# The first loads on two queues and one epsilon on VectorE, in a fused layernorm, linear attention and gated layer

## Chip, cores and metric

The kernel runs on one core of a Trainium2 chip. The metric is the device time of one execution in microseconds (us). A core has five engines: TensorE (PE, matrix products), VectorE (DVE), ScalarE (ACT), GpSimd (POOL) and SyncE (SP, which here only issues transfers). They run their own instruction streams in order and wait for one another through semaphores. Transfers between HBM and the on-chip memory are done by 16 DMA engines; an engine that issues one puts it on its queue and goes on.

## What is computed

x is 2048 tokens by 512 channels in bf16. With xn = layernorm(x) the output is x + A(xn) + B(xn):

```python
xn = (x - mean(x)) / sqrt(var(x) + 1e-5)
# A: 32 heads of 16 channels, a learned feature map, linear attention
q, k, v = split(xn @ wqkv)
phi(t) = concat(softmax(t @ w_phi), softmax(-(t @ w_phi)))
o = phi(q) @ (phi(k)^T v) / (phi(q) @ sum(phi(k)) + 1e-6)
A = o @ wo
# B: bilinear gated layer, 512 -> 1792 -> 512
B = ((xn @ w_gate) * (xn @ w_up)) @ w_down
```

## The kernel before

The tokens are cut into 16 tiles of 128 (n = 0 to 15), four tiles to a group (GT = 4). Tile n lies in `xall[:, n, :]`, one token to a partition. Everything stays on chip: all weights are loaded once, and xn is kept transposed (channels on partitions) in `xnT`, which is what the projections and the gated layer read.

The order of the work on each engine is written out by hand (`manual_schedule`, L102): the instructions of an engine stand in the order in which the program emits them. All loads are issued by SyncE in one list ahead of that (L84 to L99): tile 0, tile 1, tiles 2 and 3, two halves of wv, the first two column blocks of w_gate and w_up (`dma_gu(0, 2)`), wphi, the next two blocks, the transposed k weights (wT2), and then the rest. Eight semaphores serve the loads in turn, so that the ninth load waits for the first, and so on.

While the first tile is on its way, TensorE runs ten matmuls on zeros (`warm_up`, L305 to L309), VectorE clears some buffers, GpSimd builds an identity matrix and a block mask, and ScalarE loads its activation table and runs one Exp on a constant (L106).

The layernorm of the first four tiles is done tile by tile:

- `ln_sums` (L153): bn_stats on VectorE (L155), tile `stats`.
- bn_aggr on VectorE (L347), tile `mv`: mean and variance.
- `ln_rstd` (L162): on GpSimd, variance plus epsilon (L164, tile `ve`), then the power of -0.5 (L166, tile `rstd`).
- `ln_apply` (L169): on VectorE, (x - mean) * rstd (L171, tile `xn`).

`first_stats` and `first_apply` (L340 to L355) set the order of these on VectorE: bn_stats and bn_aggr of tile 0, bn_stats and bn_aggr of tile 1, apply of tile 0, bn_stats of tile 2, apply of tile 1, bn_aggr of tile 2, and so on.

TensorE then transposes the tile (`lt`, L210 to L215): four transposes into PSUM (`tp`), which ScalarE copies into `xnT` (in two halves for tiles 0 and 1). Then come the v projection of tile 0 (`vproj`, L315; tile `pv`, L240), with the transposes of tile 1 put between its first two and its last two matmuls, that of tile 1, and the first units of the gated layer (`unit`, L268; tiles `g` and `u`, L275), which for the first two column blocks are done in two halves of tokens. After that the main loop mixes gated units, k, q and v projections, feature maps and the attention sums, so that TensorE always has matmuls at hand; tiles 4 to 15 are normalized in the background (`ln_block`) by VectorE, GpSimd and ScalarE and transposed by DMA. A last stage does the attention of each tile and the down projection (`fin`).

Of the kernel before, what the change touches and what calls it, by code (L numbers as in the profile page):

```python
# [11 lines left out]
ALU = mybir.AluOpType  # L12
# [9 lines left out]
def kernel(  # L22
# [12 lines left out]
    nc = tc.nc  # L35
    P = 128
# [7 lines left out]
    EPS = 1e-5  # L44
# [5 lines left out]
    def token_views(ap):  # L50
        rows = ap.flatten_outer_dims()
        first = rows[0:TT, :].rearrange("(n p) d -> p n d", p=P)
        rest = rows[TT:S, :].rearrange("(p n) d -> p n d", p=P)
        return lambda lo, hi: first[:, lo:hi, :] if hi <= GT else rest[:, lo - GT:hi - GT, :]

    x_view = token_views(A_x)
# [6 lines left out]
    xall = xpool.tile([P, NT, D], BF16)  # L63
# [10 lines left out]
    def dma_x(lo, hi):  # L74
        nc.sync.dma_start(out=xall[:, lo:hi, :], in_=x_view(lo, hi))
# [5 lines left out]
        dma_cols(nc.sync, wg, B_w_gate, lo * P, hi * P)  # L81
        dma_cols(nc.sync, wu, B_w_up, lo * P, hi * P)

    dma_x(0, 1)  # L84
    dma_x(1, 2)
    dma_x(2, 4)
    for lo in (0, 2):
        nc.sync.dma_start(out=wv[:, lo:lo + 2, :],
                          in_=A_wqkv[lo * P:(lo + 2) * P, 2 * D:3 * D].rearrange("(c p) f -> p c f", p=P))
# [58 lines left out]
    def bank(name, dt=F32, n=TT):  # L148
        return ps_s.tile([P, n], dt, name=name, tag="s")
# [3 lines left out]
    def ln_sums(n):  # L153
        stats = lnpool.tile([P, nc.vector.BN_STATS_DIM], F32, name="stats")
        nc.vector.bn_stats(out=stats[:], in_=xall[:, n, :])  # L155
        return stats
# [2 lines left out]
        stats = ln_sums(n)  # L159
        nc.vector.bn_aggr(out=mv, in_=stats[:])  # L160

    def ln_rstd(mv, k):  # L162
        ve = lnpool.tile([P, GT], F32, name="ve")
        nc.gpsimd.tensor_scalar(out=ve[:, 0:k], in0=mv[:, 0:k, 1], scalar1=EPS, scalar2=None, op0=ALU.add)  # L164
        rstd = lnpool.tile([P, GT], F32, name="rstd", bufs=GT)
        nc.gpsimd.tensor_tensor(out=rstd[:, 0:k], in0=ve[:, 0:k], in1=mhalf[:, 0:k], op=ALU.pow)  # L166
        return rstd

    def ln_apply(n, mean, rstd):  # L169
        xn = xnpool.tile([P, D], BF16, name="xn")  # L170
        nc.vector.tensor_scalar(out=xn[:], in0=xall[:, n, :], scalar1=mean, scalar2=rstd,  # L171
                                op0=ALU.subtract, op1=ALU.mult)
        xns[n] = xn

    def mv_tile():
        return lnpool.tile([P, GT, nc.vector.BN_AGGR_DIM], F32, name="mv", bufs=GT)
# [33 lines left out]
    def lt(n, parts=1):  # L210
        tp = bank("tp", BF16).rearrange("p (c t) -> p c t", c=DC)
        for c in range(DC):
            nc.tensor.transpose(out=tp[:, c, :], in_=xns[n][:, c * P:(c + 1) * P], identity=ident[:])  # L213
        for c in range(0, DC, DC // parts):
            nc.scalar.copy(out=xnT[:, c:c + DC // parts, n * P:(n + 1) * P], in_=tp[:, c:c + DC // parts, :])  # L215
# [3 lines left out]
    def make_bd():  # L219
        bo, wp = BO[:], wphi[:]  # L220
        nc.vector.tensor_tensor(out=bd[:], in0=_bcast_ap(bo, [bo.ap[0], [0, DC], [E1, 8], [1, DH]]),
                                in1=_bcast_ap(wp, [wp.ap[0], [DH, DC], [0, 8], [1, DH]]), op=ALU.mult)
# [15 lines left out]
    def proj(ps, n, w, js=range(DC)):  # L238
        for j in js:
            nc.tensor.matmul(ps, lhsT=xnT[:, j, n * P:(n + 1) * P], rhs=w[:, j, :],  # L240
                             start=(j == 0), stop=(j == DC - 1))

    def features(n, w, name):
        pf = bank(name)
        proj(pf, n, w)
        e = epool.tile([P, NG, 2, 4 * DH], F32, name="e")
        pfv = pf.rearrange("p (g c) -> p g c", g=NG)
        nc.scalar.activation(out=e[:, :, 0, :], in_=pfv, func=AF.Exp, scale=1.0)  # L248
        nc.scalar.activation(out=e[:, :, 1, :], in_=pfv, func=AF.Exp, scale=-1.0)  # L249
        ev = e[:].rearrange("p g s (h f) -> p (g s h) f", f=DH)  # L250
        sums = epool.tile([P, 2 * H], F32, name="sums")
        nc.vector.tensor_reduce(out=sums[:], in_=ev, axis=AX.X, op=ALU.add)  # L252
        rs = epool.tile([P, 2 * H, 1], F32, name="rs")
        nc.vector.reciprocal(out=rs[:].rearrange("p a b -> p (a b)"), in_=sums[:])  # L254
        phi = epool.tile([P, NG, P], BF16, name=f"phi{name}")
        nc.gpsimd.tensor_tensor(out=phi[:].rearrange("p g (x f) -> p (g x) f", f=DH), in0=ev,  # L256
                                in1=rs[:].to_broadcast((P, 2 * H, DH)), op=ALU.mult)
        return phi
# [52 lines left out]
    with tc.tile_pool(name="ps_k", bufs=1, space=PSUM) as ps_k:  # L311
        kvps = [ps_k.tile([P, 4, 4, E1], F32, name=f"kv{b}") for b in range(2)]
        phiks = {}

        def vproj(n, copy=nc.scalar.copy, amid=None, later=False):  # L315
            ps = bank("pv")
            proj(ps, n, wv, range(2))
            if amid is not None:
                amid()
            proj(ps, n, wv, range(2, DC))  # L320
            def evict():
                copy(out=vts[n % NV][:, :, :, 0:DH], in_=ps.rearrange("p (a b c) -> p a b c", a=8, b=4))  # L322
            if later:
                return evict
            evict()

        def kproj(n):
            phiks[n] = features(n, W1k, "k")

        def kv(n):  # L330
            vt, phik = vts[n % NV], phiks[n]
            for gr in range(NG):
                nc.tensor.matmul(kvps[gr // 4][:, gr % 4, :, :].rearrange("p a b -> p (a b)"),  # L333
                                 lhsT=phik[:, gr, :], rhs=vt[:, gr, :, :].rearrange("p a b -> p (a b)"),
                                 start=(n == 0 and gr % 4 == 0), stop=(n == NT - 1 and gr % 4 == 3))

        mvs = [mv_tile() for n in range(GT)]
        rstds = []

        def first_apply(n):  # L340
            ln_apply(n, mvs[n][:, 0, 0:1], rstds[n][:, 0:1])

        def first_stats(n, amid=None):
            stats = ln_sums(n)
            if amid is not None:
                first_apply(amid)
            nc.vector.bn_aggr(out=mvs[n][:, 0, :], in_=stats[:])  # L347
            rstds.append(ln_rstd(mvs[n], 1))

        first_stats(0)  # L350
        first_stats(1)
        first_apply(0)
        first_stats(2, amid=1)
        first_stats(3, amid=2)
        first_apply(3)  # L355
        make_bd()
        nc.gpsimd.tensor_tensor(out=M4[:], in0=BO[:, 0:4, :], in1=BO[:, 4:8, :], op=ALU.add)
        lt(0, parts=2)
        warm_up(1)
        vproj(0, amid=lambda: lt(1, parts=2))  # L360
        copy_v = vproj(1, later=True)
        lt(2)
        copy_v()
        unit(0, 0, 0, 2 * P)
        vproj(2, copy=nc.vector.tensor_copy, amid=lambda: lt(3))
        unit(0, 1, 0, 2 * P)
        vproj(3, copy=nc.vector.tensor_copy)
        for f in range(2):
            unit(0, f, 2 * P, TT)
        del units[0:2]  # L370
        ffn(1)
        for j0 in (0, 2):
            fold(1, W1k, j0, (nc.scalar.copy, nc.vector.tensor_copy))
        ffn(1)
        ln_block(4)
        ffn(1)
        chore(2)
        kproj(0)
        ffn(1)
        chore(2)  # L380
        ffn(1)
        chore()
        kproj(1)
        ffn(1)
        chore()
        ffn(1)
        kproj(2)
        chore()
        ffn(1)
        kv(0)  # L390
        chore()
        ffn(1)
        kproj(3)
        chore()
        ffn(1)
        kv(1)
        nc.sync.dma_start(out=wT2[:, 0, :, :], in_=A_wqkv[:, 0:D], transpose=True)
        for n in range(GT, NT):
            if n in (4, 8):
                ln_block(n + 4)  # L400
            vproj(n)
            kproj(n)
            chore(1 if n % GT < 2 else 0)
            ffn(1)
            kv(n - 2)
            chore((1, 2, 2, 2)[n % GT])
            if n >= 8 and n % 2 == 0:
                qproj((n - 8) // 2)
            if n == 6:
                fold(0, W1q, 0)  # L410
            ffn(1)
            if n == 6:
                fold(0, W1q, 2)
        ffn(1)
        kv(NT - 2)
        ffn(1)
        kv(NT - 1)
        for b in range(2):
            nc.vector.tensor_tensor(out=KV[:, 4 * b:4 * b + 4, :, :], in0=kvps[b][:],
                                    in1=_bcast_ap(M4[:], [M4[:].ap[0], [0, 4], [E1, 4], [1, E1]]), op=ALU.mult)  # L420
        qproj(4)
        ffn(1)
# [64 lines left out]
```

## Time and profile before

| | |
|---|---|
| median of 3 runs | 222.05 us (221.95 to 222.31) |
| the profiled execution | 221.94 us, of which the span of its instructions is 220.2 us |
| TensorE busy | 214.5 us (97% of the span) |
| VectorE busy | 138.4 us (63%) |
| ScalarE busy | 88.2 us (40%) |
| GpSimd busy | 72.1 us (33%) |
| DMA, mean over the span | 90 GB/s, 19.91 MB |

How to read the profile: one execution was recorded instruction by instruction. Times count from the first instruction of the span. PE stands for TensorE's matmuls, PEld for its weight loads, SPq for the instructions with which SyncE issues transfers. L155 is line 155 of the kernel before. The chain of work is followed back from the last instruction: at each step to whatever released it. "issue" in it is time in which the engine waited for nothing that the profile shows. A transfer is issued, moves its packets, and lands when its semaphore has its full count.

### The profile page before, as it was taken

Reading aid. Unit: us, or ns where it says so; the run is one execution under the profiler, and the core shown is the slowest. Engines: PE = TensorE matmul, PEld = TensorE weight load, DVE = VectorE, ACT = ScalarE, POOL = GpSimd, SP = SyncE. Lnnn points to the kernel's source line nnn. Section 1 sums busy time; section 2 is a strip of 40 time slices with the busy share of each in tenths; the row PEclk is TensorE's granted clock in tenths of the full one; section 3 lists DMA queues with packets and bytes.
Section 4 is the critical chain, followed back from the end, with each engine's and each line's share of the span. In section 5 each row is a group of like instructions: output and inputs, shape, how many; then the busy total and the mean of one; then the engine's idle time right before and its main releaser. Section 6 shows DMA issues by size and latency. Waiting matters only on the chain.

```text
span 220.2 us, 3489 instructions
## 1 busy us (share of the span) xinstructions
PE 214.5 (97%) x1285; PEld 104.4 (47%) x1309; DVE 138.4 (63%) x237; ACT 88.2 (40%) x162; POOL 72.1 (33%) x62
## 2 busy tenths in 40 slices
PE   7999999999999999999999999999999999999995
PEld 2564444445444444444544444444444444454443
DVE  5657985885579685756589964197655745445321
ACT  2635486559755876545354221231322323100000
POOL 5300555455336653536333633033033033000000
PEclk9999999999999999999999999999999999999999
DMA  5999994404201223010205945214431431522611
GB/s 171 261 306 383 368 225 59 95 1 49 49 0 33 42 54 65 18 34 0 48 1 100 119 95 113 58 24 95 98 72 24 95 71 27 91 53 71 69 30 48
DMA packets 47233, 19.91 MB, mean 90 GB/s; under 512 B 37488, under 2 KB 46960, under 8 KB 47088
## 3 DMA queue, kind: packets, MB, share of 16 engines
q1 hardware_dynamic: 47216, 19.69, 39.6%
q8 instruction: 10, 0.16, 0.3%
q14 instruction: 7, 0.06, 0.1%
HBM read 8.67 MB, written 2.10 MB: 49 GB/s over the span
## 4 chain that ended last, share of the span: by engine, by line
PE 94%; DVE 2%; DMA 1%; issue 1%; POOL 0%; ACT 0%; DVEq 0%
PE fin L293 22%; PE u L275 22%; PE g L275 21%; PE fin L296 6%; PE pv L240 6%; PE q L240 6%; PE k L240 6%; PE ab L430 2%; PE kv L333 2%; DMA xall<-in_A_x_dram 1%; DVE stats L155 1%; PE pq L231 1%; DVE sums L252 1%; PE tp L213 0%; DVE hT L280 0%
## 5 line engine op out<-in xcount | busy, mean ns | idle before, releaser
L275 PE MATMUL u<-xnT,wu 128*128 128x512 bf16 (+1 forms) x229 | 57.7, 372 | 0.4
L275 PE MATMUL g<-xnT,wg 128*128 128x512 bf16 (+1 forms) x222 | 56.7, 371 | 0.4
L280 DVE TENSOR_TENSOR hT<-u,g_sb 128x512 bf16<-128x512 f32 (+1 forms) x58 | 37.4, 649 | 27.3 <-PE u L275 18.0
L279 ACT CAST g_sb<-g 128x512 bf16<-128x512 f32 (+1 forms) x58 | 33.3, 573 | 48.2 <-PE g L275 48.1
L252 DVE TENSOR_REDUCE sums<-e 128x64 f32<-128x1024 f32 x32 | 38.9, 1215 | 20.7 <-ACT e L249 20.7
L293 PE MATMUL fin<-wd,hT 128*128 128x512 bf16 (+2 forms) x234 | 50.9, 366 | 0.3
L256 POOL TENSOR_TENSOR phiq<-e,rs 128x1024 bf16<-128x1024 f32 x16 | 31.0, 1935 | 61.4 <-DVE rs L254 53.1
L256 POOL TENSOR_TENSOR phik<-e,rs 128x1024 bf16<-128x1024 f32 x16 | 30.9, 1934 | 48.2 <-DVE rs L254 46.2
L275 PEld LDWEIGHTS <-wu 128*128 128x128 bf16 x232 | 22.6, 98 | 25.7
L293 PEld LDWEIGHTS <-hT 128*128 128x128 bf16 x238 | 22.4, 98 | 24.8
L275 PEld LDWEIGHTS <-wg 128*128 128x128 bf16 x232 | 21.9, 98 | 23.4
L240 PEld LDWEIGHTS <-xnT 128*128 128x128 bf16 x192 | 17.3, 97 | 18.2 <-ACT xnT L215 1.1
L299 DVE TENSOR_TENSOR o_sb<-fin,xall 128x512 bf16<-128x512 f32 (+2 forms) x17 | 11.2, 656 | 22.3 <-PE fin L296 22.2
L248 ACT ACTIVATE e<-q 128x512 f32<-128x512 f32 x16 | 9.5, 596 | 26.1 <-PE q L240 20.7
L254 DVE RECIPROCAL rs<-sums 128x64 f32<-128x64 f32 x32 | 17.7, 553 | 3.1
L240 PE MATMUL pv<-wv,xnT 128*128 128x512 bf16 x62 | 16.4, 379 | 0.4 <-ACT xnT L215 0.2
L296 PE MATMUL fin<-wo,oT 128*128 128x512 bf16 (+2 forms) x68 | 16.6, 366 | 0.0
L240 PE MATMUL k<-W1k,xnT 128*128 128x512 bf16 x63 | 16.2, 379 | 0.0
L240 PE MATMUL q<-W1q,xnT 128*128 128x512 bf16 x60 | 15.9, 378 | 0.1
L322 ACT CAST vt<-pv 128x512 bf16<-128x512 f32 x14 | 8.3, 591 | 10.9 <-PE pv L240 10.9
L248 ACT ACTIVATE e<-k 128x512 f32<-128x512 f32 x16 | 9.6, 597 | 7.0 <-PE k L240 6.6
L439 DVE TENSOR_TENSOR otok<-ab,rden 128x512 bf16<-128x512 f32 x16 | 11.1, 691 | 0.6
(46 smaller groups left out, 117.4 us busy)
## 6 DMA issues: line engine op xcount, KB each, us to landing
out_dram<-o_sb SPq DMA_DIRECT2D x15, 128.0 KB, 1.9
wd<-in_B_w_down_dram SPq DMA_DIRECT2D x1, 1792.0 KB, 15.4
wg<-in_B_w_gate_dram SPq DMA_DIRECT2D x2, 640.0 KB, 7.0
wu<-in_B_w_up_dram SPq DMA_DIRECT2D x2, 640.0 KB, 8.1
xall<-in_A_x_dram SPq DMA_DIRECT2D x1, 1024.0 KB, 12.0
wv<-in_A_wqkv_dram SPq DMA_DIRECT2D x2, 256.0 KB, 3.9
wg<-in_B_w_gate_dram SPq DMA_DIRECT2D x2, 256.0 KB, 4.9
wu<-in_B_w_up_dram SPq DMA_DIRECT2D x2, 256.0 KB, 5.3
```

Source lines behind the costliest of these rows:

```text
L240: nc.tensor.matmul(ps, lhsT=xnT[:, j, n * P:(n + 1) * P], rhs=w[:, j, :], start=(j == 0), stop=(j == DC - 1))
L248: nc.scalar.activation(out=e[:, :, 0, :], in_=pfv, func=AF.Exp, scale=1.0)
L252: nc.vector.tensor_reduce(out=sums[:], in_=ev, axis=AX.X, op=ALU.add)
L254: nc.vector.reciprocal(out=rs[:].rearrange("p a b -> p (a b)"), in_=sums[:])
L256: nc.gpsimd.tensor_tensor(out=phi[:].rearrange("p g (x f) -> p (g x) f", f=DH), in0=ev, in1=rs[:].to_broadcast((P, 2 * H, DH)), op=ALU.mult)
L275: nc.tensor.matmul(ps, lhsT=w[:, c, f * P:(f + 1) * P], rhs=xnT[:, c, T * TT + lo:T * TT + hi], start=(c == 0), stop=(c == DC - 1))
L279: nc.scalar.copy(out=g_sb[:, 0:hi - lo], in_=pss[0])
L280: nc.vector.tensor_tensor(out=hTs[T][:, f, lo:hi], in0=pss[1], in1=g_sb[:, 0:hi - lo], op=ALU.mult)
L293: nc.tensor.matmul(ps, lhsT=hTs[T][:, f, t4 * P:(t4 + 1) * P], rhs=wd[:, f, lo:lo + w], start=(f == 0), stop=False)
L296: nc.tensor.matmul(ps, lhsT=oTs[n][:, c, :], rhs=wo[:, c, lo:lo + w], start=False, stop=(c == DC - 1))
L299: nc.vector.tensor_tensor(out=o_sb[:], in0=ps, in1=xall[:, n, lo:lo + w], op=ALU.add)
L439: nc.vector.tensor_tensor(out=o_tok[:].rearrange("p (b h d) -> p b h d", b=2, d=DH), in0=abv[:, :, :, 0:DH], in1=rden[:].to_broadcast((P, ...
```

## The change

Tile 0 is loaded by two transfers of 64 partitions each, the first issued by SyncE and the second by ScalarE. Tile 1 is loaded by one transfer issued by ScalarE, behind that half. All other loads stay on SyncE in their order. For tile 0 alone the addition of epsilon is done by VectorE, directly behind its bn_aggr; the power stays on GpSimd. Both issues on ScalarE stand ahead of its table load. No arithmetic changes.

```diff
-    dma_x(0, 1)
-    dma_x(1, 2)
+    for eng, rows in ((nc.sync, slice(0, P // 2)), (nc.scalar, slice(P // 2, P))):
+        eng.dma_start(out=xall[rows, 0, :], in_=x_view(0, 1)[rows, 0, :])
+    nc.scalar.dma_start(out=xall[:, 1, :], in_=x_view(1, 2)[:, 0, :])
     dma_x(2, 4)
...
-    def ln_rstd(mv, k):
+    def ln_rstd(mv, k, eng=nc.gpsimd):
         ve = lnpool.tile([P, GT], F32, name="ve")
-        nc.gpsimd.tensor_scalar(out=ve[:, 0:k], in0=mv[:, 0:k, 1], scalar1=EPS, scalar2=None, op0=ALU.add)
+        eng.tensor_scalar(out=ve[:, 0:k], in0=mv[:, 0:k, 1], scalar1=EPS, scalar2=None, op0=ALU.add)
...
-        def first_stats(n, amid=None):
+        def first_stats(n, amid=None, eng=nc.gpsimd):
             stats = ln_sums(n)
             if amid is not None:
                 first_apply(amid)
             nc.vector.bn_aggr(out=mvs[n][:, 0, :], in_=stats[:])
-            rstds.append(ln_rstd(mvs[n], 1))
-
-        first_stats(0)
+            rstds.append(ln_rstd(mvs[n], 1, eng))
+
+        first_stats(0, eng=nc.vector)
         first_stats(1)
```

## The prediction

> **What bounds the kernel now.** I read the shares of the chain first, then the chain's first 7 us in order of time, then the same microseconds on each engine, then the landings of the loads. All times are from the profiled execution: span 220.2 us, device time 221.94 us, so 1.74 us lie around the span. The median of the runs is 222.05 us, 0.11 above it; I add that back at the end.
>
> The shares of the chain, by engine:
>
> ```profile
> PE 94%; DVE 2%; DMA 1%; issue 1%; POOL 0%; ACT 0%; DVEq 0%
> ```
>
> TensorE is the bound; some 6% of the chain is not TensorE. The chain in order of time (start, duration, what) shows where nearly half of that lies:
>
> ```profile
> 0.79 2.09 DMA xall<-in_A_x_dram
> 2.88 0.02 issue
> 2.90 0.71 DVE stats L155
> 3.61 0.02 issue
> 3.63 0.19 DVE mv L347
> 3.82 0.08 issue
> 3.90 0.25 POOL ve L164
> 4.15 0.07 issue
> 4.22 0.59 POOL rstd L166
> 4.81 0.03 issue
> 4.84 0.42 DVE xn L171
> 5.26 0.05 issue
> 5.31 0.41 PE tp L213 x4
> 5.72 0.02 issue
> 5.74 0.38 ACT xnT L215
> 6.12 0.05 issue
> 6.17 0.60 PE pv L240 x2
> ```
>
> Until 6.17 the end is set by tile 0 alone: its load, its statistics, the epsilon and the power on GpSimd, its normalization, its transposes and the first copy out of PSUM. From 6.17 on TensorE runs to 217.4 us almost without a hole, the larger apparent ones being matmuls whose records are missing. So a microsecond saved ahead of 6.17 is one saved at the end, if nothing else holds TensorE in the next 10 us.
>
> Two loads nearly do. The first half of pv for tile 0 needs the first piece of wv, the second half (6.99) the second, and u at 8.99 needs wu. Their issues (start, duration):
>
> ```profile
> 0.79 1.35 SPq L75 DMA_DIRECT2D xall<-in_A_x_dram  x3
> 2.18 0.98 SPq L88 DMA_DIRECT2D wv<-in_A_wqkv_dram  x2
> 3.20 0.47 SPq L78 DMA_DIRECT2D wg<-in_B_w_gate_dram  x1
> 3.72 0.51 SPq L78 DMA_DIRECT2D wu<-in_B_w_up_dram  x1
> ```
>
> The landing events of the trace put wv's pieces at 5.69 and 6.95, wg at 7.86, wu at 8.92. TensorE was free at 6.84 and took the second half of pv at 6.99, 0.04 after wv landed; but it then stood 0.04 for the copies of tile 1 (L215, 7.03 to 7.41) and began pv for tile 1 at 7.46. So the late wv cost nothing in the end: it could be later by only 0.02. u follows g without a hole at 8.995, and wu could have been 0.03 later. Any gain on tile 0's chain therefore counts only if wv and wu come earlier by nearly as much.
>
> **The change, part by part.**
>
> *Epsilon on VectorE.* It removes from GpSimd's path the 0.25 of L164 and a hop of 0.08. The power starts 0.09 after its input. VectorE has no 128x1 tensor_scalar in this trace; I bound it between the memset of 128x4 (62 ns) and the bn_aggr of 128x2 or the tensor_scalar of 128x32 (180 ns), and take 0.12, between two rows equally near. mv ends at 3.81; the epsilon starts 0.04 later (bn_aggr starts 0.03 after bn_stats), runs 3.85 to 3.97; the power runs 4.06 to 4.64 and would let xn go at 4.68, 0.16 before 4.84. But the epsilon stands on VectorE ahead of tile 1's bn_stats, and xn of tile 0 stands behind tile 1's bn_stats and bn_aggr:
>
> ```profile
> 3.63 0.18 DVE L347 BATCH_NORM_AGGREGATE mv<-stats 128x2 f32<-128x6 f32 x1
> 3.73 0.66 DVE L155 BATCH_NORM_STATS2 stats<-xall 128x6 f32<-128x512 bf16 x1
> 4.42 0.18 DVE L347 BATCH_NORM_AGGREGATE mv<-stats 128x2 f32<-128x6 f32 x1
> 4.84 0.41 DVE L171 TENSOR_SCALAR xn<-xall,mv,rstd 128x512 bf16<-128x512 bf16 x1 [0.23 <-POOL rstd L166]
> ```
>
> An instruction here can start 0.10 after bn_aggr started. Tile 1's bn_stats thus goes from 3.73 to 3.95, ends at 4.61, its bn_aggr starts at 4.65, and xn of tile 0 at 4.75. VectorE, not GpSimd, is late next: **0.09 us** gained of 0.33 taken out. Bounds: 0.16 if a dependent epsilon costs VectorE less, 0.00 if it takes 0.18 and nothing starts beneath it. Tile 1's own power moves from 5.09 to about 5.2 and its xn from 5.77 to 5.86, ended 6.25; TensorE wants it at about 6.4, so that is covered by 0.15.
>
> *Tile 0 in halves.* Each half is 64 KB. The issue takes 0.40 on SP, the first packets run at 1.82, each of the 16 engines needs 8 packets of 46 ns (0.37), the last engines finish near 2.5 and the last landing comes at 2.88. The halves use the same engines, so the 0.37 stays; what can shrink is the issue and the stagger of about 0.28 between the engines' first packets, each queue now preparing 64 rows and not 128. I take half of the stagger less something for the wait for the later of two: **0.10 us**. Bounds: the page's median of 1.9 us to landing for a 128 KB store against 1.4 for a 32 KB one allows 0.4 at most; a loss is priced under the rivals.
>
> The row above says that engine time is a small part of the 2.09. The Trainium skill, "DMA: Bandwidth & Descriptors", section "Rules for kernel authors", speaks against this part: two transfers to disjoint partition halves are not worth it, since both use the same 16 engines and serialize. By that rule this term is zero and the sum falls to the epsilon's 0.09; the 0.10 rests on latency outside the engines.
>
> *Tile 1 and x(2,4).* Tile 1's issue goes to ScalarE, second there, at about 1.24, as on SP now. bn_stats wants it at 3.95 less the 0.10; it now lands at 3.39. Beside x(2,4), which shares the engines from its first packet, it may lose the 0.35 that its own bytes take: 3.74. Just covered; if it came after 3.85 every 0.1 would delay xn of tile 0 by 0.1, since xn is behind that bn_stats.
>
> *The other loads.* All loads behind tile 1 on SP are issued one slot, 0.46, earlier. At present data waits for issues: by the trace's DMA packets the engines stand almost idle from 2.95 to 3.3 (10 KB in a quarter of a microsecond, against 96 at the busiest). The bytes ahead of wv and wu are the same, so closing that hole brings them 0.2 to 0.46 earlier, enough for a gain of 0.19 on the chain. wphi now waits for a half of tile 0 before its issue near 3.8; that landed a microsecond before.
>
> *ScalarE.* Two issues of 0.4 to 0.46 precede the table load (1.28 at 0.78 now), which then ends near 3.0, the first Exp at 3.2. The next work is L215 at 5.74: 2.5 us of cover, so nothing.
>
> **Sum.** 0.09 + 0.10 = 0.19 us off the profiled 221.94: 221.75; with the 0.11 of the median, **221.86 us**. TensorE's ten warm-up matmuls cap it: the last starts at 4.74 and takes 0.22, so tile 0's transposes, now at 5.31, cannot start before about 4.97, a cap of 0.34.
>
> About 0.2% (0.44 us) is what a measurement of this kernel can tell from no change. My forecast is within it.
>
> **Rivals.**
>
> *Halves bring nothing.* Both halves land at 2.88 as the one did. Only the epsilon counts: 222.05 - 0.09 = 221.96. For it: shared engines. Against: only 0.37 of 2.09 is engine time.
>
> *Chain gains up to the cap.* The halves land 0.25 or more sooner: 222.05 - 0.34 = 221.71.
>
> *The loads were the cost in the timed runs.* wv and wu stand 0.02 and 0.03 from holding TensorE in the execution profiled, and the runs reach 222.31, 0.37 over it. If ordinary runs lose 0.2 to 0.37 to a late wv or wu, the earlier issues remove it beside the chain's 0.19 to 0.34: 222.05 - 0.45 to 0.65, about 221.5. Against it: the median is only 0.11 above the profiled run.
>
> *ScalarE's queue is served late (the slower side).* First packets of the first three DMAs appear at 1.82, 2.59 and 3.3, 0.7 to 0.77 apart though issued 0.46 apart. If something common to both queues hands out DMAs at that pace, the second half of tile 0 starts near 2.59 and lands between 3.2 and 3.39, and tile 1, fourth in turn, at 4.2 to 4.5. xn of tile 0 then starts 0.25 to 0.65 later: 222.3 to 222.7, say 222.5. It decides from a landing of tile 0 past 2.97 or of tile 1 past 3.95. Against it: the engines take 96 KB in 0.25 us once fed, so no common pace of that size holds later.
>
> **Numbers.** Forecast 0.36, halves bring nothing 0.12, cap 0.08, loads 0.24, late queue 0.20, of which 0.04 stays within 0.2%. Faster is the loads' 0.24; slower 0.16; same 0.60. The range runs from 221.45, leaving out the best of the loads' case, to 222.50, leaving out the worse half of the late queue.
>
> **What would show it.** Right: tile 0's later half landing at 2.7 to 2.85; the power on GpSimd following VectorE by 0.09; xn of tile 0 near 4.65 directly behind tile 1's bn_aggr; first pv near 5.98 and TensorE full from there; wv and wu landing by 6.75 and 8.75. Wrong: VectorE waiting for tile 1's load; TensorE waiting at the second half of pv or at u; xn still waiting for the power; or the time around the span growing from 1.74 with a second queue in use.

## The result and the profile after

The changed kernel takes 222.55 us (median of 19 runs, 222.35 to 222.98) against 222.28 us before (19 runs, 221.95 to 222.64): a ratio of 1.0014, 95% interval [1.0008, 1.0021]. It is slower by about 0.3 us where 0.19 less was forecast, and lies 0.05 above the range. Part of the distance is the kernel before itself: over these 19 runs its median is 222.28, 0.23 above the 222.05 of three runs from which the forecast was reckoned. The sign is wrong by either count.

The profiled execution of the changed kernel took 222.98 us, the longest of its runs (span 221.2), while that of before was among the shortest of its own. The two traces differ by 1.04 us, the medians by 0.27, so the traces show where time goes, not how much of it. Each kernel was therefore profiled once more below (`before_again`, `after_again`).

The chain of waits of the changed kernel in its first profile (start, duration, what):

```profile
1.40 3.38 DMA xall<-in_A_x_dram
...
4.80 0.71 DVE stats L156
...
5.71 0.31 DVE xn L172
...
7.14 0.61 PE pv L241 x2
```

In this execution the chain runs through tile 1, not tile 0: a load of 3.38 us on ScalarE's queue, then bn_stats, bn_aggr and only then xn of tile 0. The first pv starts at 7.14 and not at 6.17. The same seen on VectorE, idle time ahead of an instruction in brackets:

```profile
3.22 0.69 DVE L156 BATCH_NORM_STATS2 stats<-xall 128x6 f32<-128x512 bf16 x1 [1.34 <-DMA xall<-in_A_x_dram]
...
4.80 0.69 DVE L156 BATCH_NORM_STATS2 stats<-xall 128x6 f32<-128x512 bf16 x1 [0.48 <-DMA xall<-in_A_x_dram]
...
5.62 0.38 DVE L172 TENSOR_SCALAR xn<-xall,mv,rstd 128x512 bf16<-128x512 bf16 x1
```

Tile 0's bn_stats starts at 3.22 against 2.90, and tile 1's waits 0.48 for its load. The issues, on SyncE and on ScalarE, in the same profile:

```profile
0.79 0.58 SPq L85 DMA_DIRECT2D xall<-in_A_x_dram  x1
1.42 0.57 SPq L75 DMA_DIRECT2D xall<-in_A_x_dram  x1
2.05 0.96 SPq L89 DMA_DIRECT2D wv<-in_A_wqkv_dram  x2
...
0.79 0.57 ACTq L85 DMA_DIRECT2D xall<-in_A_x_dram  x1
1.40 0.68 ACTq L86 DMA_DIRECT2D xall<-in_A_x_dram  x1
```

Half a tile is issued in 0.57 to 0.58 us where a whole one took 0.40, and the issues behind the halves are slow as well (0.68 on ScalarE, 0.57 on SyncE from 1.42). wv, which was to move from 2.18 to 1.72, moved to 2.05.

How the start carries to the end: the first pv of tile 1 starts at 7.46 in the first profile of before (221.94 us), 7.61 in its second (222.11), 8.26 and 8.43 in the two of the changed kernel (222.79 and 222.98), 8.73 in `e5_xn0_first` (223.29). The difference is 214.5 to 214.6 each time. In the other eleven profiles it is 214.4 to 214.9, most where wu came late and held u as well (`e7_halves_both_on_sp`, `e11_tiles23_halves`). Nearly all that follows is TensorE at work; the changed kernel's loss is made in the first 8 us.

### The profile page after: what moved, and what is told of

It reads as the page before. It is cut to its first block, busy times and chain, and to the rows that moved or that the text cites. A ratio compares the mean times of both kernels' runs of the same rounds, so it can differ in the third digit from the quotient of the medians.

```text
span 221.2 us, 3515 instructions
## 1 busy us (share of the span) xinstructions
PE 216.7 (98%) x1309; PEld 104.7 (47%) x1309; DVE 138.6 (63%) x238; ACT 88.1 (40%) x162; POOL 71.9 (32%) x61
## 4 chain that ended last, share of the span: by engine, by line
PE 96%; DMA 2%; DVE 1%; ACTq 0%; issue 0%
PE g L276 22%; PE fin L294 22%; PE u L276 22%; PE pv L241 6%; PE fin L297 6%; PE q L241 6%; PE k L241 6%; PE ab L431 2%; PE kv L334 2%; DMA xall<-in_A_x_dram 2%; PE tp L214 1%; PE pq L232 1%; DVE stats L156 0%; ACTq L85 0%; PE warm L308 0%; DVE xn L172 0%
## 5 line engine op out<-in xcount | busy, mean ns | idle before, releaser
L276 PE MATMUL g<-xnT,wg 128*128 128x512 bf16 (+1 forms) x232 | 57.9, 372 | 0.0
L156 DVE BATCH_NORM_STATS2 stats<-xall 128x6 f32<-128x512 bf16 x16 | 10.7, 669 | 1.8 <-DMA xall<-in_A_x_dram 1.8
```

What stands on the lines that cost most here:

```text
L276: nc.tensor.matmul(ps, lhsT=w[:, c, f * P:(f + 1) * P], rhs=xnT[:, c, T * TT + lo:T * TT + hi], start=(c == 0), stop=(c == DC - 1))
```

## The experiments

The first theory, drawn from the two traces, was Q: two queues that issue at once slow each other, and tile 1 comes late behind that. Two rivals stood against it: V, the epsilon itself delays VectorE, and C, the moment at which TensorE's clock rises makes the whole difference. "The clock rises" is short here for what the traces show of matmuls of 512 columns: up to some moment they start 0.43 us apart, and 0.22 apart after it. Every ratio is to the kernel before, run on the same chip. Code is cut to the lines that differ from the changed kernel, unless the text names the kernel before.

**The epsilon alone** (`e1_eps_only`): loads as before.

```diff
-    for eng, rows in ((nc.sync, slice(0, P // 2)), (nc.scalar, slice(P // 2, P))):
-        eng.dma_start(out=xall[rows, 0, :], in_=x_view(0, 1)[rows, 0, :])
-    nc.scalar.dma_start(out=xall[:, 1, :], in_=x_view(1, 2)[:, 0, :])
+    dma_x(0, 1)
+    dma_x(1, 2)
```

> All loads as before, only tile 0's epsilon on VectorE. Theory Q (the queues: two queues issuing at once take longer for each issue, and tile 1, second on ScalarE's queue, lands so late that VectorE waits for it ahead of xn of tile 0): this part is harmless, xn of tile 0 some 0.03 to 0.1 us earlier than before's 4.84, time 0.0 to 0.15 below before. Rival V (the epsilon ahead of tile 1's bn_stats delays VectorE by more than it saves): time 0.1 to 0.3 above before, VectorE the last to arrive at xn. Rival C (the profiled difference is TensorE's clock turning at another moment): no difference.

Measured: 222.29 against 222.30, ratio 1.0003 [0.9993, 1.0012]. This part loses nothing that can be told. The interval alone would leave room for V's 0.1 to 0.27 us, but on the chain the epsilon did what was forecast: xn of tile 0 starts 1.86 after tile 0's landing, against 1.96 in both profiles of before, so 0.10 is gained and V falls; the epsilon takes 154 ns on VectorE. But TensorE in this profile:

```profile
1.24 4.45 PE L307 MATMUL warm<-zeros 128*128 128x512 bf16 x10 [1.24 <-DVE zeros L104]
5.48 0.63 PE L213 MATMUL tp<-ident,xn 128*128 128x128 bf16 x4
```

The ten warm-ups end only here, at 5.48, with starts 0.43 apart to the last; xn was ready at 5.23 and waited. In the first profile of before they ended at 4.96: the ninth starts at 4.52, the tenth 0.22 behind it.

**The loads alone** (`e2_loads_only`): `first_stats(0)` without `eng=nc.vector`.

> The loads of the changed kernel, epsilon of all tiles on GpSimd. Theory Q: the whole loss is here, time 0.25 to 0.45 above before, tile 1 landing past 4.3 and bn_stats of tile 1 waiting for it. Rival V: time at or below before, since the loads would be the gain. Rival C: no difference.

Measured: 222.63, ratio 1.0017 [1.0008, 1.0027]. The loss is in the loads. But tile 1 landed at 3.84 and held nobody; tile 0 was complete only at 3.66, 0.78 later than in the first profile of before. So tile 1's 4.77 of the first profile after did not recur here, and tile 0 itself is late. Of Q's two signs the time came and the late tile 1 did not.

**Tile 1 back on SyncE** (`e3_tile1_on_sp`): halves as changed.

```diff
-    nc.scalar.dma_start(out=xall[:, 1, :], in_=x_view(1, 2)[:, 0, :])
+    dma_x(1, 2)
```

> Tile 0 in halves on the two queues, tile 1 back on SyncE behind its half; epsilon on VectorE. Theory Q: tile 0 still lands near 3.2 (its issues still meet), but tile 1, now ahead of tiles 2 and 3, lands by 3.6 to 3.8 and VectorE no longer waits for it; xn of tile 0 near 5.0; time 0.0 to 0.2 above before. If the late half of tile 0 is what costs and not tile 1: as the changed kernel, 0.25 to 0.4 above before. Rival V: 0.1 to 0.3 above before.

Measured: 223.03, ratio 1.0037 [1.0025, 1.005], worse than both, and more than any theory had asked. Tile 0 was complete at 3.20; VectorE no longer waited for tile 1, and the loss stayed. SyncE's second issue took 0.83 though ScalarE issued nothing beside it any more, wv went out at 2.81 and its second piece landed at 7.71. The chain has the first half of pv and its second half, which starts 0.04 after that landing and 1.25 behind the first half's start, where in before it was 0.82. The chain names ScalarE's copy of tile 1, which ended at the same moment, but this half reads tile 0 and wv:

```profile
6.50 0.60 PE pv L241 x2
...
7.75 1.46 PE pv L241 x6
```

**xn of tile 0 ahead of tile 1's statistics** (`e5_xn0_first`).

```diff
-        first_stats(1)
         first_apply(0)
+        first_stats(1)
```

> The changed kernel with xn of tile 0 placed on VectorE ahead of tile 1's bn_stats, so that nothing of tile 0 stands behind tile 1's load. Theory Q: tile 0's chain is then load, bn_stats, bn_aggr, epsilon, power, xn without a wait for tile 1: xn at about 5.0 against 5.62, and the time 0.1 to 0.35 below the changed kernel, unless tile 1's transposes then hold TensorE. Rival V: the same gain, for another reason, but e1 then is slower than before. Rival C: no difference to the changed kernel.

Measured: 223.29, ratio 1.0049 [1.0036, 1.0062], the slowest of all: a miss. xn of tile 0 came at 5.14 as expected, but tile 1's bn_stats stood behind it, its xn started at 7.40, and tile 1's transposes, between the two halves of pv, at 7.87. Tile 1 had landed at 3.93, so here there was no wait for its load to remove; the order costs more than it saves.

**Tile 0 whole on SyncE, tile 1 on ScalarE** (`e4_tile1_alone_on_act`).

```diff
-    for eng, rows in ((nc.sync, slice(0, P // 2)), (nc.scalar, slice(P // 2, P))):
-        eng.dma_start(out=xall[rows, 0, :], in_=x_view(0, 1)[rows, 0, :])
+    dma_x(0, 1)
     nc.scalar.dma_start(out=xall[:, 1, :], in_=x_view(1, 2)[:, 0, :])
```

> Tile 0 whole on SyncE, only tile 1 on ScalarE's queue, where it is first; epsilon on VectorE. Theory Q as it now stands (two issues made at once take 0.55 to 0.58 us and not 0.40, a next one on SyncE up to 0.83, so the slot that SyncE was to save is lost): SyncE's first two issues take 1.1 to 1.4 together, wv is issued at 2.05 to 2.3 and not 1.71; tile 1 lands by 3.4 together with tile 0, so VectorE doesn't wait for it; time between before and the changed kernel, 222.2 to 222.5. If a second queue in itself, not the meeting of issues, is the loss: as the changed kernel, 222.5 or more.

Measured: 222.76, ratio 1.002 [1.0011, 1.0029], as the expectation had it if a second queue in itself is the loss. Q's mechanism falls. The issues on both queues meet, and none is slow:

```profile
0.79 0.88 SPq L75 DMA_DIRECT2D xall<-in_A_x_dram  x2
1.72 0.97 SPq L88 DMA_DIRECT2D wv<-in_A_wqkv_dram  x2
...
0.79 0.39 ACTq L85 DMA_DIRECT2D xall<-in_A_x_dram  x1
```

First packets appear at 1.83 and 1.92 on the two queues. Still tile 0 lands late:

```profile
0.79 2.62 DMA xall<-in_A_x_dram
```

In before that line read 2.09. The packets of the two tiles run over the same stretch, from 1.83 to 3.05, and tile 0's last one comes at 3.00 against 2.53 in the first profile of before; both tiles finish late (3.41 and 3.60). The trace doesn't say which engine moved a packet, so that the two wait for each other on the engines is argued from these times, in one profile. wv left at 1.72, yet its second piece landed at 7.17: the earlier issue bought nothing.

**Both halves on SyncE** (`e7_halves_both_on_sp`): one queue only.

```diff
-    for eng, rows in ((nc.sync, slice(0, P // 2)), (nc.scalar, slice(P // 2, P))):
-        eng.dma_start(out=xall[rows, 0, :], in_=x_view(0, 1)[rows, 0, :])
-    nc.scalar.dma_start(out=xall[:, 1, :], in_=x_view(1, 2)[:, 0, :])
+    for rows in (slice(0, P // 2), slice(P // 2, P)):
+        nc.sync.dma_start(out=xall[rows, 0, :], in_=x_view(0, 1)[rows, 0, :])
+    dma_x(1, 2)
```

> Tile 0 in halves, both on SyncE, all other loads behind them there; epsilon on VectorE. Theory Q: with one queue each issue takes 0.40 again, also for half a tile; tile 0's second half is issued at 1.25 and lands near 3.2 to 3.4; all later loads one slot (0.46) later, so that wv's second piece lands near 7.3 and holds TensorE; time 0.2 to 0.5 above before. If a half issues and lands in clearly less than a whole (1.5 to 1.8 us after its issue): tile 0 complete by 2.9, time within 0.2 of before.

Measured: 223.20, ratio 1.0034 [1.0022, 1.0046]. The chain shows each issue:

```profile
0.79 0.58 SPq L85
...
1.42 0.57 SPq L85
...
2.04 0.59 SPq L75
...
2.68 0.42 SPq L75
```

With no second queue in use a half takes 0.58, and the issue right behind the halves, a whole tile, 0.59. The first half's first packet runs at 2.14 against 1.82, and it lands at 2.96: 64 KB alone arrive no earlier than 128 KB did. Part of the time lost here is the extra slot: wu landed at 10.12 and held u until 10.17, 0.3 after TensorE had come free. This gave theory H: a transfer of 64 partitions is slow in itself.

**Tile 0 cut by columns** (`e9_column_halves`), all else as changed.

```diff
-    for eng, rows in ((nc.sync, slice(0, P // 2)), (nc.scalar, slice(P // 2, P))):
-        eng.dma_start(out=xall[rows, 0, :], in_=x_view(0, 1)[rows, 0, :])
+    for eng, cols in ((nc.sync, slice(0, D // 2)), (nc.scalar, slice(D // 2, D))):
+        eng.dma_start(out=xall[:, 0, cols], in_=x_view(0, 1)[:, 0, cols])
```

> The changed kernel with tile 0 cut by columns (128 partitions x 256) and not by partitions. Theory H (a transfer of 64 partitions is itself slow to issue, 0.57 against 0.40 us, and brings its first packet 0.3 later, whatever the other queue does): each issue takes 0.40 or less, first packets near 1.85, tile 0 complete by 2.75 to 3.0, wv issued at 1.7; tile 1 lands between 3.4 and 3.9; time 222.1 to 222.45, at least 0.1 under the changed kernel. Rival S (two queues slow each other on the engines, however the tile is cut): tile 0 complete at 3.2 or later, time as the changed kernel's.

Measured: 222.44, ratio 1.0010 [1.0001, 1.0019]. Issues and first packets are as H says:

```profile
0.79 0.40 SPq L85 DMA_DIRECT2D xall<-in_A_x_dram  x1
1.24 0.44 SPq L75 DMA_DIRECT2D xall<-in_A_x_dram  x1
```

First packets run at 1.83 and 1.89. Tile 0 was complete at 3.15, later than H expected, perhaps since tile 1 and tiles 2 and 3 follow on two queues; tile 1 landed at 3.85. The time is below the changed kernel's as H asks, but the two intervals overlap, so the gain of 0.1 is not shown by the times alone.

**Column halves, tile 1 on SyncE, xn of tile 0 amid tile 1's statistics** (`e10_column_halves_amid`).

```diff
-    for eng, rows in ((nc.sync, slice(0, P // 2)), (nc.scalar, slice(P // 2, P))):
-        eng.dma_start(out=xall[rows, 0, :], in_=x_view(0, 1)[rows, 0, :])
-    nc.scalar.dma_start(out=xall[:, 1, :], in_=x_view(1, 2)[:, 0, :])
+    for eng, cols in ((nc.sync, slice(0, D // 2)), (nc.scalar, slice(D // 2, D))):
+        eng.dma_start(out=xall[:, 0, cols], in_=x_view(0, 1)[:, 0, cols])
+    dma_x(1, 2)
...
-        first_stats(1)
-        first_apply(0)
+        first_stats(1, amid=0)
```

> Tile 0 in column halves on the two queues, tile 1 back on SyncE behind its half, epsilon on VectorE, xn of tile 0 between tile 1's bn_stats and bn_aggr. Theory H: all loads but the second column half run as before, tile 0 complete by 2.75 to 2.9, tile 1 at about 3.4; time 221.9 to 222.2, the lowest so far, if halving can bring anything; 222.15, as with whole tiles in this order, if it can't. Rival S: tile 0 past 3.1, time above 222.3.

Measured: 222.66, ratio 1.0012 [1.0003, 1.0021]: a miss for H's hopeful side. Tile 0 was complete at 3.08, the half on SyncE last (its first packet at 2.11 against 1.81 on ScalarE). That is nearer to S (past 3.1, above 222.3) than to H. It also shows a first packet 0.3 late with all 128 partitions, so the late packet is not the partitions' alone when two queues are in use. Halving brings nothing even in the cheap form; in this profile wv's second piece landed at 7.53 and held pv besides.

**Tiles 2 and 3 in partition halves** (`e11_tiles23_halves`): the kernel before with only its third load cut.

```diff
-    dma_x(2, 4)
+    for rows in (slice(0, P // 2), slice(P // 2, P)):
+        nc.sync.dma_start(out=xall[rows, 2:4, :], in_=x_view(2, 4)[rows, :, :])
```

> The kernel before, tiles 0 and 1 whole on SyncE as ever, and only the third load (tiles 2 and 3) cut into two transfers of 64 partitions, both on SyncE: 128 KB each, as much as tile 0 whole. Theory H (the number of partitions makes an issue slow): both issues take 0.55 to 0.6 us, the issues behind them 0.75 later than before, wv's second piece past 7.5, time 0.3 to 0.8 above before. Rival B (what was slow was a small transfer, or the first one on an idle queue): 0.40 to 0.43 each, time 0.1 to 0.4 above before from one more slot.

Measured: 222.80, ratio 1.0025 [1.0012, 1.0038]. The chain, from the second issue on:

```profile
1.23 0.42 SPq L75
...
1.70 0.73 SPq L87
...
2.47 0.60 SPq L87
...
3.11 0.60 SPq L89
...
3.75 0.47 SPq L89
```

The halves carry 128 KB each and stand behind two whole tiles, and take 0.73 and 0.60; one more whole issue behind them is slow (0.60), then it is 0.47 again. The 0.73 is more than H's 0.55 to 0.6. Neither a small size nor first use makes an issue slow: with tiles 2 and 3 whole (128 partitions, 256 KB) it took 0.43, so the cut to 64 partitions does. wu landed 0.44 later than in the first profile of before, at 9.36, and held u until 9.41. That wv's second piece would come past 7.5 was a miss: 6.99.

**Both kernels once more** (`before_again`, `after_again`).

> The kernel before once more, one look. Theory W (the moment at which TensorE's clock rises differs between executions and makes most of before's spread): the ten warm-ups run at 0.43 us until a rise at some other moment than 4.4; if the rise comes after 5.5, tile 0's transposes start at 5.48 and not when xn is ready, and the time is 222.2 to 222.6; tile 0 lands again between 2.85 and 3.0.

> The changed kernel once more, one look. Theory H: halves issued in 0.57, tile 0 complete at 3.0 to 3.7, wv issued past 2.0. If the clock rises earlier than in the first profile (7.0), the time is 222.35 to 222.6, with xn of tile 0 still 0.4 or more behind before's. Rival C (the whole difference between the first two profiles is the clock): xn of tile 0 near 4.9.

Measured: 222.11 and 222.79. Before again, tile 0's transposes on TensorE:

```profile
5.46 0.39 PE L213 MATMUL tp<-ident,xn 128*128 128x128 bf16 x4
```

Tile 0's bn_stats and xn, before and after:

```profile
2.94 0.69 DVE L155 BATCH_NORM_STATS2 stats<-xall 128x6 f32<-128x512 bf16 x1 [1.05 <-DMA xall<-in_A_x_dram]
...
4.87 0.41 DVE L171 TENSOR_SCALAR xn<-xall,mv,rstd 128x512 bf16<-128x512 bf16 x1 [0.23 <-POOL rstd L166]
```

```profile
3.50 0.69 DVE L156 BATCH_NORM_STATS2 stats<-xall 128x6 f32<-128x512 bf16 x1 [1.62 <-DMA xall<-in_A_x_dram]
...
5.34 0.38 DVE L172 TENSOR_SCALAR xn<-xall,mv,rstd 128x512 bf16<-128x512 bf16 x1
```

Before, the transposes start at 5.46 though xn was ready at 5.28: the tenth warm-up, begun at the low rate at 5.05, came first, and the clock rose while it ran. After again, the first matmuls of pv:

```profile
6.98 0.59 PE L241 MATMUL pv<-wv,xnT 128*128 128x512 bf16 x2 [0.17 <-DMA wv<-in_A_wqkv_dram]
```

The clock thus rose at another moment than 4.4, as W has it, though not late enough for the 222.2 named. In after again the halves took 0.58 and 0.55 to issue, wv went out at 2.30, and the clock rose between 6.2 and 7.0. Tile 0 was complete at 2.91 before and 3.40 after; xn of tile 0 started at 4.87 and 5.34, 0.47 apart; rival C, which wanted 4.9, falls as the whole cause. pv then waited 0.17 for wv's first piece, which landed at 6.94 (5.80 before), so that in this execution the loads behind tile 0 cost too. Tile 1 landed at 3.72 and held nobody.

**What the clock hides** (`e8_before_8_warmups`, `e6_xn0_amid`, `e12_amid_9_warmups`). The first is the kernel before with `warm_up(8)`; the other two have before's loads, the epsilon on VectorE, and

```diff
-        first_stats(1)
-        first_apply(0)
+        first_stats(1, amid=0)
```

the last of them with `warm_up(9)`.

> The kernel before with 8 in place of 10 warm-up matmuls. Theory W (in ordinary executions TensorE's clock rises late, the warm-ups run at 0.43 us each until 5.5 and cover tile 0's chain up to there; the profiled execution of before was one with an early rise): the end of the warm-ups moves to 4.65, the median falls by 0.05 to 0.3, the fastest stay. Rival: the warm-ups never bind, and two fewer either change nothing or let the clock rise later: median equal or above.

> Loads as before, epsilon on VectorE, and xn of tile 0 placed between tile 1's bn_stats and bn_aggr. xn of tile 0 then waits for the power and comes 0.16 us before where it stood against tile 0's landing. If the ten warm-up matmuls at the low clock, which end at 5.48 in some executions, hide such gains: median 0.0 to 0.1 below before, the fastest runs 0.1 or more below before's fastest. If VectorE's chain is the bound in ordinary runs: 0.15 below before throughout.

> Loads as before, epsilon on VectorE, xn of tile 0 amid tile 1's statistics, and 9 in place of 10 warm-ups. Theory W (the end of the warm-ups covers what tile 0's chain gains): the warm-ups end by 5.05 at the latest, tile 0's transposes start 0.05 behind xn in every execution, median 0.1 to 0.3 below before. Rival: the clock rises later for the missing one and takes it back, or some executions near 224 as with 8 warm-ups: median 0.1 below before or less.

Measured: 222.19, ratio 1.0010 [0.9990, 1.0029], with three runs of twelve at 223.7 to 224.0; 222.13, ratio 0.9995 [0.9987, 1.0004]; 222.14, ratio 0.9995 [0.9986, 1.0004]. None can be told from before. In `e6_xn0_amid` xn started 1.83 after tile 0's landing, 0.13 better than before. In `e12_amid_9_warmups` the transposes did start close behind xn, at 5.22, but ran at the low clock:

```profile
5.22 0.61 PE L213 MATMUL tp<-ident,xn 128*128 128x128 bf16 x4
...
6.29 0.94 PE L240 MATMUL pv<-wv,xnT 128*128 128x512 bf16 x2
```

pv of tile 1 began at 7.91 nonetheless. So W holds for what it says of the warm-ups' end, and fails in that taking one away frees the time: in this profile real work then runs at the low rate instead. No version here beats before clearly.

## Why the prediction was wrong, point by point

- **The bound.** Right: what happens ahead of the first pv carries to the end one for one, as the differences of 214.5 show, as long as wu doesn't hold u behind it.
- **The epsilon, 0.09.** Right on the chain (0.10 measured, with VectorE and not the power as the last), and worth nothing in the time that can be told (1.0003). What hid it in `e1_eps_only`'s profile is the warm-ups' end at 5.48. The text had the cap at 4.97, from one execution whose clock rose early, between the starts at 4.20 and 4.52; in the fifteen other profiles it rose later in all but one (`e11_tiles23_halves`, between 4.20 and 4.44), up to about 7 (`e12_amid_9_warmups`). The timed runs were not divided by their clock, so how much it hides in the median is not shown.
- **Tile 0 in halves, 0.10 us.** This is the step that failed. It took the issue and the stagger of the engines' first packets to shrink with the rows, though before's own issues hardly do (0.40 to 0.41 for one tile, 0.43 for two). Its outer bound came from stores that all had 128 partitions. Issued by partitions, a half takes 0.55 to 0.58 and not 0.40. Its first packet comes 0.32 later with one queue in use, and on the later of two queues 0.54 to 0.59 later (2.36 to 2.41 against 1.82). It lands no earlier than the whole. Where SyncE's half is last, the wait for two landings adds another 0.08. Tile 0 was complete at 2.88 to 2.99 in the six profiles with whole tiles on one queue and the early loads untouched, and at 3.20 to 3.66 in the five with partition halves on two queues: 0.2 to 0.8 lost where 0.1 was to be gained. The cheap cut by columns gave 3.08 and 3.15. The rule of the Trainium skill ("DMA: Bandwidth & Descriptors", section "Rules for kernel authors") that two transfers to disjoint partition halves don't pay, which the prediction weighed and set aside, pointed the right way; the measured 0.2 to 0.8 later is worse than the zero that the prediction drew from it.
- **Tile 1, "just covered" at 3.74.** It landed at 3.72 to 3.93 in four profiles with it second on ScalarE, and held nobody; only the first profile after had it at 4.77, with a wait of 0.48. But two of the four are past the 3.85 that the prediction allowed: the cover held because tile 0 itself was late.
- **The other loads, one slot earlier.** Wrong twice. The slow issues gave the slot back (wv at 2.05 to 2.31 in the four profiles with the changed loads, against 2.18). And where the slot was truly saved (`e4_tile1_alone_on_act`, `e9_column_halves`: 1.72 and 1.73) wv's second piece landed at 7.17 and 6.66, against 6.56 to 7.23 in the six profiles with the early loads as before: no gain that can be told. The hole in the transfers at 2.95 to 3.3 was misread: the engines were not idle for want of an issue. In the first trace of before 16 packets that start from 2.81 to 3.10 take 0.35 to 0.58 us each, where most take 0.046, so few new bytes start while they run. In the two profiles that saved the slot the hole was filled (380 and 293 GB/s from 2.95 to 3.30, against 53 to 146 in the six), and wv came no earlier. What sets its landing is not shown.
- **ScalarE.** Right: the table load ended at 3.39, the first copy came at 6.71. The time around the span did not grow: 222.98 less the trace's 221.24 is 1.74, as before.
- **Rivals.** "ScalarE's queue is served late" had nearly the measured time (222.5) and the right first sign, tile 0 past 2.97, but not the mechanism; its nearness is luck. In four of the five profiles with partition halves on two queues it is SyncE's half that landed last, and the two queues' first packets were 0.22 to 0.27 apart, not 0.7 to 0.77. Whole tiles on two queues issue in 0.39 each and start 0.09 apart (`e4_tile1_alone_on_act`). The row behind it was misread as well: tile 0 has 128 packets of 1 KB, and in the first trace of before the 129th starts at 2.40 and the 257th at 2.96, so tile 1 and tiles 2 and 3 were under way before 2.59 and 3.3. It was given 0.20 and priced half of its spread outside the range.

Two costs are shown, then: partition halves (on one queue in `e7_halves_both_on_sp` and `e11_tiles23_halves`), and a second queue whose packets run beside tile 0's (`e4_tile1_alone_on_act`); tile 0 is late in every profile in which either touches its load. Why it is late is argued. How the changed kernel's 0.27 divides between them is not settled: `e9_column_halves` takes the first away and is lower by 0.1, within the intervals. How much of it is the later loads, which held pv in `after_again`, is not settled either. Why 64 partitions issue slowly stays open too; no other count was tried.

## What to carry to other kernels

Before cutting a first load in halves, look at what its time is made of: here 0.37 of 2.09 us was engine work, and the rest didn't shrink with the bytes. On this evidence, keep all 128 partitions in each early transfer, and keep other queues quiet until the transfer that everything waits for has landed. And read a start-up phase in more than one execution: a margin of 0.3 us seen once may belong to the moment at which the clock rose.

## What the runs showed of the hardware that was not expected

- A transfer of 64 partitions was issued in 0.55 to 0.73 us, one of 128 of the same or twice the bytes in 0.39 to 0.47, and the next issues behind halves took 0.57 to 0.83 before returning to 0.43 to 0.47 (`e7_halves_both_on_sp`, `e11_tiles23_halves`, `e3_tile1_on_sp`).
- The time from issue to landing of tile 0's partition halves, 2.1 to 2.9 us, was that of a whole tile alone on its queue (2.1 to 2.2) or longer.
- bn_stats, which waits for both halves' semaphores, started 0.02 after the last landing when ScalarE's half was last and 0.10 after it when SyncE's was (3.22 after 3.195; 3.50 after 3.403). In the trace of the changed kernel the wait for SyncE's half is an instruction of its own ahead of bn_stats, and that for ScalarE's half is bn_stats' own.
- TensorE's matmuls of 512 columns start 0.43 us apart until some moment between 4.2 and about 7 us, and 0.22 apart after it. In the two profiles of the kernel before, with the same instructions ahead, it lies between the starts at 4.20 and 4.52 and between those at 5.05 and 5.46. The profile's granted clock, 1.0 in these spans, doesn't show it; the starts do.
